# The layer norm's 1/std by three Newton steps on VectorE, in place of Sqrt on ScalarE and a reciprocal

**Chip, cores, metric.** One core of a Trainium2 chip. The metric is the device time of one execution in microseconds (us); the profiles' spans are about 1.8 us shorter.

## The reference, cut to what matters

```python
def _attn_ref(q, k, v, tau):                      # 8 batches, 8 heads, 576 tokens, head size 64
    scores = scale * np.matmul(q, k.transpose(0, 1, 3, 2))
    thresh = np.max(scores, axis=-1, keepdims=True) - tau
    scores = np.where(scores >= thresh, scores, -1000000000.0)
    ... softmax, then attn @ v

def _moe_ref(x, g_ln, w_ch1, w_ch2):              # x: (8, 576, 512), the attention's output
    mu = np.mean(x, axis=-1, keepdims=True)
    var = np.mean((x - mu) ** 2, axis=-1, keepdims=True)
    xn = (x - mu) / np.sqrt(var + 1e-06) * g_ln
    ch = np.maximum(xn @ w_ch1, 0.0) @ w_ch2      # 512 -> 2048 -> 512
    return (x + ch).astype(np.float32)
```

## The kernel before

The work is 72 *slots* of attention (9 for each batch, about 18.5 us each) and 16 *groups* of 288 tokens of the feed-forward part. TensorE runs matmuls of a group between the matmuls of the slots; each slot has four quarters in which such steps are issued. 1/std is a factor of a whole token, so it is applied after the second matmul, and may come late. The tiles that matter: `sc` (scores, PSUM), `em` (attention weights, turned by way of DRAM: `et` to `scr` to `em`), `hidden` (the 2048 features, evicted by ScalarE from one of two PSUM buffers), `rb` (1/std). L numbers in the profiles are lines of the whole kernel.

```python
def exponentials():
    ...
    for h in range(2):
        nc.vector.tensor_reduce(out=neg[:, i], in_=sc[h]..., op=ALU.max, negate=True)        # L372
        nc.gpsimd.tensor_scalar(out=thr[:, i], in0=neg[:, i], ...)
    for i in range(4):
        if i == 2:
            yield es, thr
        nc.scalar.activation(es[:, i], blocks[i], func=AF.Exp, bias=neg[:, i : i + 1])       # L383

def weights(es, thr):
    for i in range(4):
        nc.vector.scalar_tensor_tensor(out=es[:, i], in0=blocks[i], scalar=thr..., in1=es[:, i], ...)  # L389, masking
    nc.vector.reciprocal(den, den)
    for i in range(4):
        nc.gpsimd.tensor_scalar(out=es[:, i], in0=es[:, i], scalar1=den[:, i : i + 1], ...)  # L395, dividing

def ffn_steps(g):
    for d in range(ND):
        ...                                       # four products into p1
        nc.scalar.activation(hidden[:, d], p1, func=AF.Relu)                                 # L587
        yield 2
        ...
        if d == 8:
            var = ps_ff.tile([128, TOK], F32, tag="ff", name="var")
            product(var, lhsT=avg_sb, rhs=sq[:, 0], start=True, stop=True)
            rb = ffn.tile([128, TOK], F32, tag="rb", bufs=2, name="rb")
            nc.scalar.activation(rb, var, func=AF.Sqrt, bias=eps_sb)                         # L598
            aside.append(lambda: nc.vector.reciprocal(rb, rb))                               # L599
            yield 1
    ...

# one slot n, cut to its order
scores(b, s)
rest = exponentials(); es, thr = next(rest)       # maxima and two exponentials
...; second_part(n, 0); next(rest, None)          # quarter 0 of the group's steps, two exponentials
...; run_all(aside); ...; second_part(n, 1)
weights(es, thr)
run_all(aside); ...; second_part(n, 2)
scr = turn_blocks(s, es)                          # L453 and the write to DRAM; fetched in the next slot
...; run_all(aside); ...; second_part(n, 3); tick(4)
run_all(aside)
```

`run_all(aside)` runs what is in the list at that moment; what is appended meanwhile waits for the next call.

Of the kernel before, what the change touches and what calls it, by code (L numbers as in the profile page):

```python
# [10 lines left out]
I32 = mybir.dt.int32  # L11
I64 = mybir.dt.int64
ALU = mybir.AluOpType
AF = mybir.ActivationFunctionType
# [4 lines left out]
def kernel(  # L19
# [31 lines left out]
    nc = tc.nc  # L51
# [29 lines left out]
    eps_sb = consts.tile([128, 1], F32, name="eps_sb")  # L81
# [13 lines left out]
    def product(out, lhsT, rhs, **flags):  # L95


        for h in range(2):
            r = slice(64 * h, 64 * h + 64)
            nc.tensor.matmul(out[r], lhsT=lhsT[:, r], rhs=rhs, **flags)  # L100
# [20 lines left out]
    def load_v(u):  # L121
# [13 lines left out]
        out=tau_sb, in_=bass.AP(tensor=tau.tensor, offset=tau.offset, ap=[[0, 128], [1, 1]])  # L135
    )
    load_qk(0, (nc.sync, nc.scalar))
    for t in q_diag + rests + v_rest:
# [9 lines left out]
        out=scl_sb, in0=tau_sb, scalar1=0.0, scalar2=SCALE, op0=ALU.is_ge, op1=ALU.mult  # L148
    )
    nc.vector.tensor_scalar(  # L150
        out=low_sb, in0=tau_sb, scalar1=0.0, scalar2=BIG, op0=ALU.is_lt, op1=ALU.mult
    )
    nc.vector.scalar_tensor_tensor(
        out=low_sb, in0=tau_sb, scalar=-1.0, in1=low_sb, op0=ALU.mult, op1=ALU.subtract
# [385 lines left out]
    aside, stores = [], []  # L540
# [7 lines left out]
    def add_to_x(g, m, p2, rb):  # L548
        o = ffn.tile([128, TOK], F32, tag="o", bufs=6, name="o")
        nc.vector.tensor_mul(o, p2, rb)  # L550
        nc.gpsimd.tensor_tensor(out=o, in0=o, in1=groups[g][:, m], op=ALU.add)  # L551
        aside.append(lambda: store(g, m, o))
# [6 lines left out]
    def send(g, m, ot):  # L559
        b, t = divmod(g, 2)  # L560
        for i in range(4):
# [5 lines left out]
                in_=ot[32 * i : 32 * i + 32].rearrange("p (n c) -> p n c", c=32),  # L567
            )

    def ffn_steps(g):  # L570



        xc = centred.pop(g)
        rb = None
        for d in range(ND):
            while conversion.ended < 4 * (d // 4 + 1):
                yield 0
            p1 = ps_ff.tile([128, TOK], F32, tag="ff", name="p1")
            for c in range(NK):  # L580
                product(
                    p1, lhsT=w1_sb[c][:, d * 128 : (d + 1) * 128], rhs=xc[:, c],
                    start=(c == 0), stop=(c == NK - 1),
                )
                if c < NK - 1:
# [3 lines that stand above are left out]
            if d == 1:  # L589
                sq = ffn.tile([128, NK, TOK], F32, tag="sq", bufs=1, name="sq")  # L590
                nc.scalar.activation(sq, xc, func=AF.Square)  # L591
                for c in range(1, NK):
                    nc.gpsimd.tensor_tensor(out=sq[:, 0], in0=sq[:, 0], in1=sq[:, c], op=ALU.add)  # L593
            if d == 8:
                var = ps_ff.tile([128, TOK], F32, tag="ff", name="var")
                product(var, lhsT=avg_sb, rhs=sq[:, 0], start=True, stop=True)
                rb = ffn.tile([128, TOK], F32, tag="rb", bufs=2, name="rb")
                nc.scalar.activation(rb, var, func=AF.Sqrt, bias=eps_sb)  # L598
                aside.append(lambda: nc.vector.reciprocal(rb, rb))  # L599
                yield 1  # L600
        for m in range(NK):
            p2 = ps_ff.tile([128, TOK], F32, tag="ff", name="p2")
            for d in range(ND):
                while conversion.ended < conversion.n1 + d + 1:
                    yield 0
                product(
                    p2, lhsT=w2_sb[:, d, m * 128 : (m + 1) * 128], rhs=hidden[:, d],
                    start=(d == 0), stop=(d == ND - 1),
                )
                if d < ND - 1:  # L610
                    yield 2
            aside.append(lambda m=m, p2=p2: add_to_x(g, m, p2, rb))
            yield 2
# [47 lines left out]
    def group_ready(g):  # L661
        at = ready(g) - 1
        for fn in (mean_of, centre):
            at_quarter(*divmod(at, QUARTERS), fn, g)
        at_quarter(*divmod(at + 1, QUARTERS), lambda: queue.append(ffn_steps(g)))
# [108 lines left out]
```

## Time and profile before

| | before |
|---|---|
| median of the first runs | 1529.1 us |
| TensorE busy | 93% of the span |
| VectorE, ScalarE, GpSimd busy | 55%, 29%, 32% |
| table loads on ScalarE | 32 x 1.283 us |
| TensorE waits for ScalarE's evictions into `hidden` | 23.6 us in 21 places |

TensorE sets the time from 190 us on, so what counts of any other engine is how long it makes TensorE wait. The lines for this stand in the prediction.

### The profile page before, as it was taken

What the parts mean: (1) busy time and instruction counts of PE and PEld (TensorE: products, weight loads), DVE (VectorE), ACT (ScalarE), POOL (GpSimd) and SP (SyncE); (2) the same over time, 40 slices, a digit from 0 to 9 for tenths busy, and PEclk for the clock granted to TensorE, in tenths of its full rate; (3) what the DMA queues carried; (4) which work ended last, traced back from release to release, by engine and by line L of the source; (5) the groups of instructions that cost most, each with busy time, mean ns of one, the idle gap of its engine ahead of it and who ended that gap; (6) DMA issues with size and microseconds to landing.
All of it is one profiled execution on the core that took longest, in us unless ns stands there. A gap on an engine that the chain in (4) does not pass through costs nothing.

```text
span 1527.7 us, 28886 instructions
## 1 busy us (share of the span) xinstructions
PE 1416.8 (93%) x11700; PEld 833.7 (55%) x11700; DVE 837.7 (55%) x1380; ACT 442.2 (29%) x797; POOL 487.7 (32%) x737
## 2 busy tenths in 40 slices
PE   3557899999999999999999999999999999999998
PEld 1335455565555555565555655565555655565554
DVE  5877855555654566455664556455654556545210
ACT  3445531323132322314132232313222231313120
POOL 4667443222332323132331323223232323222100
PEclk8777899999999999999999999999999999999999
DMA  9611237455764577555774567645774567545300
GB/s 221 163 39 57 68 82 165 120 136 149 173 164 125 135 171 176 135 137 148 170 169 118 147 154 175 153 125 138 160 169 125 145 152 174 141 125 136 101 9 16
DMA packets 460693, 205.07 MB, mean 134 GB/s; under 512 B 275024, under 2 KB 420176, under 8 KB 460560
## 3 DMA queue, kind: packets, MB, share of 16 engines
q1 hardware_dynamic: 458160, 202.93, 54.4%
q8 instruction: 92, 1.51, 0.4%
q10 hardware_dynamic: 2368, 0.30, 0.2%
q14 instruction: 41, 0.34, 0.1%
q0 software_dynamic: 32, 0.00, 0.0%
HBM read 119.41 MB, written 83.76 MB: 133 GB/s over the span
## 4 chain that ended last, share of the span: by engine, by line
PE 83%; ACT 5%; DVE 5%; POOL 2%; issue 2%; SPq 1%; DMA 1%; POOLq 0%; ACTq 0%; DVEq 0%
PE p L100 62%; PE sc L492 10%; PE sc L359 8%; ACT e L383 4%; DVE neg L372 3%; PE sc L100 2%; POOL e L395 1%; DVE e L389 1%; SPq L112 1%; ACT hidden L587 1%; PE mean L100 1%; ACT L383 0%; DMA v_rest<-in_v_dram 0%; ACT em L423 0%; PE tr L429 0%
## 5 line engine op out<-in xcount | busy, mean ns | idle before, releaser
L100 PE MATMUL p<-xc,w 128*64 128x288 f32 x4096 | 528.5, 414 | 24.9 <-ACT hidden L587 23.6
L100 PE MATMUL p<-hidden,w 128*64 128x288 f32 x4096 | 514.2, 407 | 0.0
L100 PEld LDWEIGHTS p<-xc,w 128*64 128x64 f32 x4096 | 293.5, 139 | 239.5 <-ACT hidden L587 39.0
L100 PEld LDWEIGHTS p<-hidden,w 128*64 128x64 f32 x4096 | 291.2, 137 | 198.4 <-issue 1.4
L372 DVE TENSOR_REDUCE neg<-sc 128x2 f32<-128x1152 f32 x144 | 189.4, 1352 | 339.8 <-PE sc L359 270.0
L395 POOL TENSOR_SCALAR e<-e,den 128x576 f32<-128x576 f32 x288 | 227.3, 806 | 282.9 <-DVE den L393 263.1
L383 ACT ACTIVATE e<-sc,neg 128x576 f32<-128x576 f32 x288 | 192.7, 742 | 289.0 <-DVE neg L372 272.1
L389 DVE SCALAR_TENSOR_TENSOR e<-sc,thr,e 128x576 f32<-128x576 f32 x288 | 219.1, 813 | 26.7 <-ACT e L383 26.2
L453 DVE STREAM_TRANSPOSE et<-e 128x1152 f32<-128x1152 f32 x112 | 153.1, 1372 | 72.5 <-POOL e L395 61.5
L587 ACT ACTIVATE hidden<-p 128x288 f32<-128x288 f32 x256 | 105.1, 415 | 278.2 <-PE p L100 276.1
L359 PE MATMUL sc<-kT,qT 64*128 64x512 f32 (+3 forms) x1024 | 154.3, 439 | 22.7 <-DVE e L389 10.9
L376 POOL TENSOR_SCALAR thr<-neg,low_sb 128x2 f32<-128x2 f32 x144 | 40.3, 280 | 374.2 <-DVE neg L372 374.2
L492 PE MATMUL sc<-em,v_in 128*64 128x256 f32 (+1 forms) x1536 | 149.1, 340 | 4.8 <-DVE e L389 4.4
L359 PEld LDWEIGHTS sc<-kT,qT 64*128 64x128 f32 x1024 | 86.1, 191 | 106.2 <-issue 79.9
L492 PEld LDWEIGHTS sc<-em,v_in 128*64 128x64 f32 x1536 | 97.4, 144 | 49.2 <-DVE e L389 7.1
L509 ACT COPY x<-sc 128x256 f32<-128x256 f32 x64 | 23.9, 373 | 320.5 <-PE sc L492 320.4
L550 DVE TENSOR_TENSOR o<-p,rb 128x288 f32<-128x288 f32 x64 | 28.3, 442 | 123.1 <-PE p L100 123.1
L551 POOL TENSOR_TENSOR o<-o,x 128x288 f32<-128x288 f32 x64 | 51.1, 798 | 131.6 <-DVE o L550 131.3
L518 POOL TENSOR_TENSOR sum<-sum,x 128x256 f32<-128x256 f32 (+1 forms) x64 | 32.2, 502 | 108.2 <-ACT x L509 105.7
L593 POOL TENSOR_TENSOR sq<-sq 128x288 f32<-128x288 f32 x48 | 38.7, 807 | 45.8 <-ACT sq L591 43.3
L492 PE MATMUL sc<-rest,v_rest 128*64 128x256 f32 (+1 forms) x384 | 49.3, 336 | 0.0
L599 DVE RECIPROCAL rb<-rb 128x288 f32<-128x288 f32 x16 | 31.2, 1953 | 30.3 <-ACT rb L598 29.9
(107 smaller groups left out, 656.1 us busy)
## 6 DMA issues: line engine op xcount, KB each, us to landing
scr<-et SPq DMA_DIRECT2D x252, 288.0 KB, 5.1
em<-scr SPq DMA_DIRECT2D x63, 1024.0 KB, 5.9
q_in<-in_q_dram SPq DMA_DIRECT2D x128, 72.0 KB, 3.4
out_dram<-ot SPq DMA_DIRECT2D x256, 36.0 KB, 4.1
k_in<-in_k_dram SPq DMA_DIRECT2D x124, 72.0 KB, 2.7
v_in<-in_v_dram SPq DMA_DIRECT2D x64, 128.0 KB, 4.3
rest<-scr SPq DMA_DIRECT2D x63, 128.0 KB, 5.9
w<-in_moe_w_ch_dram SPq DMA_DIRECT2D x12, 512.0 KB, 4.8
```

The costliest lines, as they stand in the source:

```text
L100: nc.tensor.matmul(out[r], lhsT=lhsT[:, r], rhs=rhs, **flags)
L359: nc.tensor.matmul(sc[h][:, at : at + n], lhsT=qT[r, half, j * 128 : (j + 1) * 128], rhs=kT[r, o : o + n], start=True, stop=True,)
L372: nc.vector.tensor_reduce(out=neg[:, i], in_=sc[h][:, : 2 * S].rearrange("p (j n) -> p j n", j=2), axis=AXL.X, op=ALU.max, negate=True,)
L376: nc.gpsimd.tensor_scalar(out=thr[:, i], in0=neg[:, i], scalar1=-1.0, scalar2=low_sb, op0=ALU.mult, op1=ALU.add,)
L383: nc.scalar.activation(es[:, i], blocks[i], func=AF.Exp, bias=neg[:, i : i + 1])
L389: nc.vector.scalar_tensor_tensor(out=es[:, i], in0=blocks[i], scalar=thr[:, i : i + 1], in1=es[:, i], op0=ALU.is_ge, op1=ALU.mult, accum_o ...
L395: nc.gpsimd.tensor_scalar(out=es[:, i], in0=es[:, i], scalar1=den[:, i : i + 1], scalar2=1.0, op0=ALU.mult, op1=ALU.mult,)
L453: nc.vector.transpose(et[:, :, 64 * h : 64 * h + 64].rearrange("p n (j c) -> p j n c", j=2), es[:, 2 * h : 2 * h + 2].rearrange("p j (n c) ...
L492: nc.tensor.matmul(dst[64 * h : 64 * h + 64], lhsT=vt[:, c, h, :] if c < J else vr[:, h, :], rhs=pick(em[:, c] if c < J else er, hp, h), s ...
L551: nc.gpsimd.tensor_tensor(out=o, in0=o, in1=groups[g][:, m], op=ALU.add)
L587: nc.scalar.activation(hidden[:, d], p1, func=AF.Relu)
L593: nc.gpsimd.tensor_tensor(out=sq[:, 0], in0=sq[:, 0], in1=sq[:, c], op=ALU.add)
```

## The change

In the profile before, each Sqrt has a load of function tables in front of it (16), and so has the exponential that follows (15 times). A load takes 1.283 us. The intent is to do without both: ScalarE only adds the bias (Identity), and VectorE finds 1/sqrt from a guess on the float's bits and three Newton steps. Each step is put into the list of side work by the one before it, so the three parts land in three places.

```diff
+    def root(y, x, t, step=0):
+        if step == 0:
+            nc.vector.tensor_scalar(
+                out=y.bitcast(I32), in0=x.bitcast(I32), scalar1=-0.5, scalar2=float(0x5F3759DF),
+                op0=ALU.mult, op1=ALU.add,
+            )
+        nc.vector.scalar_tensor_tensor(
+            out=t, in0=y, scalar=-0.5, in1=y, op0=ALU.mult, op1=ALU.mult
+        )
+        nc.vector.tensor_mul(t, t, x)
+        nc.vector.scalar_tensor_tensor(out=y, in0=t, scalar=1.5, in1=y, op0=ALU.add, op1=ALU.mult)
+        if step < 2:
+            aside.append(lambda: root(y, x, t, step + 1))
 ...
-                nc.scalar.activation(rb, var, func=AF.Sqrt, bias=eps_sb)
-                aside.append(lambda: nc.vector.reciprocal(rb, rb))
+                nc.scalar.activation(sq[:, 1], var, func=AF.Identity, bias=eps_sb)
+                aside.append(lambda: root(rb, sq[:, 1], sq[:, 2]))
```

## The prediction

> **What bounds the kernel now.** I read the busy shares first, then the slices, the chain of waits, the waits by engine, and last the timeline around the sixteen square roots (one for each group of 288 tokens). The page, in that order:
>
> ```profile
> PE 1416.8 (93%) x11700; PEld 833.7 (55%) x11700; DVE 837.7 (55%) x1380; ACT 442.2 (29%) x797; POOL 487.7 (32%) x737
> ...
> PE   3557899999999999999999999999999999999998
> ...
> PE p L100 62%; PE sc L492 10%; PE sc L359 8%; ACT e L383 4%; DVE neg L372 3%; PE sc L100 2%; POOL e L395 1%; DVE e L389 1%; SPq L112 1%; ACT hidden L587 1%; PE mean L100 1%; ACT L383 0%; DMA v_rest<-in_v_dram 0%; ACT em L423 0%; PE tr L429 0%
> ```
>
> TensorE is at nine tenths from the sixth slice (190 us) to the end; only the start leaves it idle. In the stretch from 230 to 1414 us it is busy for 1160.4 of 1184 us, at a granted clock of 1.00. The chain runs through matmuls for over four fifths. So a change on ScalarE and VectorE is worth only the TensorE idle time it removes or adds. What is touched, from the groups of instructions:
>
> ```profile
> L598 ACT ACT_TABLE_LOAD x16 | 20.5, 1283 | 0.3
> L383 ACT ACT_TABLE_LOAD x15 | 19.2, 1283 | 43.8 <-DVE neg L372 43.8
> ...
> L599 DVE RECIPROCAL rb<-rb 128x288 f32<-128x288 f32 x16 | 31.2, 1953 | 30.3 <-ACT rb L598 29.9
> ...
> L598 ACT ACTIVATE rb<-var,eps_sb 128x288 f32<-128x288 f32 x16 | 8.0, 502 | 0.2
> ```
>
> That is 39.7 us of table loads and 31.2 us of reciprocals, on engines that are 29% and 55% busy. How much of it TensorE feels, the waits say:
>
> ```profile
> PE p L100 <- ACT hidden L587: 23.6, 21, 2.0
> ```
>
> In 21 places the first-layer matmuls wait until ScalarE has evicted an earlier product into `hidden` (two PSUM buffers turn there). In the timeline the 21 places are of three kinds. Seven are like this one, where a table load is part of the delay:
>
> ```profile
> 890.88 2.62 DVE L372 TENSOR_REDUCE neg<-sc 128x2 f32<-128x1152 f32 x2 [4.87 <-PE sc L359]
> ...
> 892.32 1.28 ACT L383 ACT_TABLE_LOAD   x1 [3.27 <-DVE neg L372]
> ...
> 893.61 1.38 ACT L383 ACTIVATE e<-sc,neg 128x576 f32<-128x576 f32 x2
> ...
> 894.88 0.41 ACT L587 ACTIVATE hidden<-p 128x288 f32<-128x288 f32 x1
> ...
> 895.34 6.04 PE L100 MATMUL p<-xc,w 128*64 128x288 f32 x48 [0.53 <-ACT hidden L587]
> ```
>
> The exponential table is fetched back only when the maximum has arrived, then two exponentials, then the eviction; TensorE sits 0.53 us (first number of a row: start, second: length; in brackets the idle time before it). Fourteen are of this kind:
>
> ```profile
> 968.82 2.64 ACT L383 ACTIVATE e<-sc,neg 128x576 f32<-128x576 f32 x4 [3.29 <-DVE neg L372]
> ...
> 971.33 0.43 ACT L587 ACTIVATE hidden<-p 128x288 f32<-128x288 f32 x1
> ...
> 971.77 1.28 ACT L598 ACT_TABLE_LOAD   x1
> 971.81 9.19 PE L100 MATMUL p<-xc,w 128*64 128x288 f32 x60 [1.97 <-ACT hidden L587]
> ```
>
> Here the wait is over four exponentials in front of the eviction; the load for Sqrt comes after it. Every second group has a gap of 1.97 us of this kind and one of 0.51 us some 19 us earlier, with no load near: 7 x 2.48 = 17.4 us, which the change doesn't touch. The rest, 23.6 - 17.4 = 6.2 us, is the seven of the first kind: five of 0.53 us and two of 1.79 us.
>
> [...] the load begins 0.03 us after its predecessor's end. [...] relu and copies follow both loads without one of their own. So Identity in place of Sqrt should leave one load in the program. [...] the trace's 128x288 operations have 442. [...] its two-input operations on 128x512 (L243) took 0.69 us at best and 1.81 at worst.
>
> **The change part by part.** *ScalarE* loses 16 + 15 loads, 39.7 us, and keeps 16 evictions of 0.50 us [...]. Expected: 442.2 - 39.7 = 402.5 us busy. On TensorE this is worth:
> - five gaps of 0.53 us: the eviction comes 1.28 us earlier, more than the gap: 5 x 0.53 = 2.7 us;
> - two gaps of 1.79 us (ending at 373.5 and 1243.9 us), where four exponentials stand before the eviction: only the 1.28 of the load goes, 2 x 1.28 = 2.6 us;
> - one load at 181.0 us in the start, ahead of the copies that a transpose waits 2.44 us for: 1.3 us;
> - a wait of 0.09 us beside the Sqrt load in every second group: 8 x 0.09 = 0.7 us.
>
> Together at most 7.2 us, 0.47% of 1529.2.
>
> *VectorE* loses the reciprocal, 1.95 us, and gets ten instructions per group: one tensor-scalar on the bits, and three times three with two tensors. The latter are 0.44 to 0.46 us each. The first has one source in SBUF; the like of it in the conversion (L239) took 0.42 us for 512 elements at best, so for 288 some 0.3 us. Sum 9 x 0.45 + 0.3 = 4.4 us in place of 1.95: 16 x 2.4 = 39 us more, 837.7 to about 877 us, 57% of the span, without contention. It still isn't the bound. What counts is where the three parts fall. They enter the queue of side work one after another, so each lands at another point of the slots (a slot is one block of attention, about 18.5 us):
> - Groups like the one at 971.8: the first part follows the attention weights, the second the block transposes, the third ends the slot. The transposes end perhaps 1.3 us later. The weights that are fetched from that slot were issued at 986.13 with a median landing of 5.9 us, and used at 1000.45: 8 us to spare. Nothing lost.
> - Groups like the one at 882.2 (Sqrt late in its slot): the first part is at the slot's end, where VectorE then idles 4.87 us: free. The second, 3 x 0.45 = 1.35 us, falls into the next slot just ahead of the masking of the weights (L389), which there starts as soon as VectorE is free (895.81): 1.35 us later. The third comes after the masking, beside GpSimd's four divisions by the sum (L395, 0.73 us each), before the transposes. VectorE waits there 1.6 us for GpSimd anyway, so without contention the third part is hidden; [...]
>
> So in every second group the turned weights reach the next slot 1.35 to 2.65 us later. They go out to DRAM and come back, and the fetch usually waits for the write:
>
> ```profile
> SPq L468 <- DMA scr<-et: 145.0, 69, 4.7
> ```
>
> In the slot after 903.5 the fetch was issued at 911.85, lands near 917.8, and TensorE uses it at 920.33: 2.5 us to spare. Over the seven such slots after the start I find from issue, landing and first use 3.6, 2.0, 2.5, 2.4, 1.2, 3.9 and 1.4 us to spare. In some the fetch itself waits a little behind other loads, and takes up 0.4 to 1.6 us of the delay. A delay of 1.35 us overruns only the last, by about 0.6 us (with TensorE 0.5 us earlier, [...]); one of 2.65 us overruns five, by 1.05, 0.2, 0.3, 0.5 and 1.9: 4 us.
>
> [...] *Buffers:* the bias sum and scratch go into slices of `sq` that are dead by then; the next group writes `sq` only some 60 us later. The first product that needs `rb` is ready some 20 us after the root begins, three parts or not (last group: 1478.4 against 1498.24).
>
> Sum: -7.2 + 0.6 to 4, that is 3.2 to 6.6 us gained. I take 4.7 us: 1524.5 us.
>
> **The rivals.** (1) *Nothing gained*: the second and third parts of the root, lengthened by GpSimd, make TensorE wait for the fetched weights as long as it no longer waits for ScalarE; or they delay the conversion in the first 230 us, where TensorE is busy 66.75 of 75 us in the stretch from 155 on. For it: spare times of 1.2 to 2 us. Against: half the groups have 8 us to spare. 1527 to 1531 us. (2) *The whole 40 us of loads come back*, as if ScalarE were on the path: about 1490 us. Against it: the waits of TensorE on ScalarE are 23.6 us in all, and 17.4 of them have no load in front. (3) *VectorE becomes the bound*, 39 us more work: 1560 us. Against: it idles 4 to 8 us in front of nearly every maximum. (4) *The full 7 us*: contention is small and every spare time suffices: 1522 us.
>
> **Range and chances.** Between (4) and (1): 1521.5 to 1529.5. Faster by 2% would need 30 us where TensorE's waits on the touched parts are 7; slower by 2% would need nearly 2 us lost in each group: 0.005 and 0.01.
>
> **What would show it.** One table load; ScalarE near 402 us busy. The gaps of 0.53 us gone, those of 1.79 down to about 0.5, so TensorE's waits on `hidden` near 18.4 us; the fourteen others unchanged. Root operations of 0.45 us at their shortest, longer where GpSimd is at work; VectorE at 877 to 900 us. New, short waits of TensorE in front of the weighted values (L492), in the slots after every second group. Wrong would be the account if these waits are absent and the time still doesn't fall, if the gaps of 0.53 us stay, or if Identity brings loads of its own.

## The result, and the profile after

The first four runs took 1523.75, 1524.8, 1526.81 and 1528.45 us: median 1525.8 against 1529.1. The ratio was 0.998, 95% interval 0.9962 to 0.9997. (A ratio is the mean time of one kernel's fast runs over that of the other's of the same rounds, so it isn't quite the ratio of the medians.) Six more runs later gave a median of 1527.89, from 1523.45 to 1530.1, ratio 0.9993 (0.998 to 1.0007). So the change gains 1 to 3 us of 1529, about 0.1 to 0.2%, and the second batch alone cannot tell it from nothing.

The busy line of the page after:

```profile
PE 1413.7 (93%) x11700; PEld 834.5 (55%) x11700; DVE 892.2 (59%) x1524; ACT 401.6 (26%) x766; POOL 491.1 (32%) x737
```

ScalarE lost 40.6 us and 31 instructions (the loads; one is left, at L247), VectorE gained 54.5 us. The waits of TensorE, longest first (total in us, times, longest one):

```profile
PE p L100 <- ACT hidden L603: 18.2, 16, 2.0
...
PE sc L492 <- DVE et L453: 1.4, 1, 1.4
```

The first is the wait for evictions, 23.6 us before: five gaps of 0.53 us are gone, and the two of 1.79 us are 0.45. The second is new, in front of the weighted values. VectorE's `et` is named there, but that transpose only ended at the same moment and is not what this matmul reads. The matmul reads `em`, fetched from DRAM, and in the trace the fetch landed 0.14 us before it, 7.8 us after its issue (the median is 5.9). In another profile of the same kernel the same wait is named by its transfer:

```profile
PE sc L492 <- DMA em<-scr: 0.5, 1, 0.5
```

Now the second group of a batch at the place that the prediction shows of before (timeline: start, length, engine, line, what, in brackets the idle time before it):

```profile
880.97 0.31 DVE L574 TENSOR_SCALAR rb<-sq 128x288 int32<-128x288 int32 x1 [0.19 <-ACT sq L614]
881.32 0.46 DVE L578 SCALAR_TENSOR_TENSOR sq<-rb 128x288 f32<-128x288 f32 x1
...
883.29 0.46 DVE L581 TENSOR_TENSOR sq<-sq 128x288 f32<-128x288 f32 x1
...
890.36 1.37 ACT L383 ACTIVATE e<-sc,neg 128x576 f32<-128x576 f32 x2 [3.29 <-DVE neg L372]
...
891.62 0.41 ACT L603 ACTIVATE hidden<-p 128x288 f32<-128x288 f32 x1
...
893.89 0.46 DVE L578 SCALAR_TENSOR_TENSOR sq<-rb 128x288 f32<-128x288 f32 x1
...
895.25 0.81 DVE L389 SCALAR_TENSOR_TENSOR e<-sc,thr,e 128x576 f32<-128x576 f32 x1
```

The exponential follows its maximum at once. Of the root, two parts lie at the end of the slot (from 880.97), where VectorE is free, and the third (from 893.89) directly in front of the masking, which it puts off by 1.36 us.

To see where time comes and goes I compared, slot by slot, when the first maximum of the slot starts in the two traces. From 250 us on the profiled run after gains 0.75 us in each of five second groups and 1.34 in two, 6.4 us together, and 0.06 us beside each former Sqrt load. It loses 1.62 us in one slot (the wait of 1.4), and 0.5 us in all in three others. The larger steps that are left, two of about +1.69 us and one of -1.70, come from something else: the granted clock. The trace shows intervals of 3.413 us at half clock, each costing 1.7 us of matmuls. Between 250 and 1500 us there are three of them before (at 624, 798 and 972 us) and four after. In the second profile of the changed kernel there are seven. Four intervals more are 6.8 us, over twice what the change gains. Before 250 us the profiled run gains 2.3 us, the second profile of the same kernel 0.7.

### The profile page after: what moved, and what is told of

It is laid out like the page before. It is cut to its first block, busy times and chain, and to the rows that moved or that the text cites. A ratio compares the mean times of both kernels' runs of the same rounds, so it can differ in the third digit from the quotient of the medians.

```text
span 1522.0 us, 28782 instructions
## 1 busy us (share of the span) xinstructions
PE 1413.7 (93%) x11700; PEld 834.5 (55%) x11700; DVE 892.2 (59%) x1524; ACT 401.6 (26%) x766; POOL 491.1 (32%) x737
## 4 chain that ended last, share of the span: by engine, by line
PE 82%; DVE 6%; ACT 4%; POOL 3%; issue 2%; DMA 2%; SPq 1%; POOLq 0%; ACTq 0%; DVEq 0%
PE p L100 61%; PE sc L492 10%; PE sc L359 8%; ACT e L383 3%; DVE neg L372 2%; POOL e L395 2%; PE sc L100 2%; DVE e L389 1%; SPq L112 1%; DMA v_rest<-in_v_dram 1%; PE mean L100 1%; DVE w L266 0%; DVE w L239 0%; DMA scr<-et 0%; ACT hidden L603 0%
## 5 line engine op out<-in xcount | busy, mean ns | idle before, releaser
L100 PE MATMUL p<-xc,w 128*64 128x288 f32 x4096 | 525.3, 413 | 19.0 <-ACT hidden L603 18.2
L395 POOL TENSOR_SCALAR e<-e,den 128x576 f32<-128x576 f32 x288 | 230.6, 817 | 287.1 <-DVE den L393 271.2
L383 ACT ACTIVATE e<-sc,neg 128x576 f32<-128x576 f32 x288 | 192.7, 741 | 337.0 <-DVE neg L372 337.0
L518 POOL TENSOR_TENSOR sum<-sum,x 128x256 f32<-128x256 f32 (+1 forms) x64 | 32.5, 508 | 92.8 <-ACT x L509 90.3
L429 PE MATMUL tr<-ident,e 128*64 128x128 f32 x36 | 9.1, 405 | 41.8 <-ACT em L423 34.1
```

What stands on the lines that cost most here:

```text
L100: nc.tensor.matmul(out[r], lhsT=lhsT[:, r], rhs=rhs, **flags)
```

## The experiments

Twelve runs (eleven new kernels and the changed one again), all with five rounds, four to six executions each. The four batches of experiments ran on different chips. Runs in one batch share the runs of before: 1529.26 us in the first batch, 1528.13 in the second, 1528.35 in the third, 1528.92 in the fourth (medians; the single runs lie between 1526.16 and 1531.11).

| run | median us | ratio, 95% interval | correct |
|---|---|---|---|
| ScalarE's half alone | 1522.3 | 0.996 (0.9948 to 0.9972) | no |
| VectorE's half alone | 1526.88 | 0.9995 (0.9982 to 1.0008) | no |
| root in one piece | 1525.94 | 0.9984 (0.9972 to 0.9997) | yes |
| changed kernel again | 1527.89 | 0.9993 (0.998 to 1.0007) | yes |
| root ahead of the masking | 1554.54 | 1.0178 (1.0155 to 1.0201) | yes |
| root behind the masking | 1553.41 | 1.0164 (1.015 to 1.0178) | yes |
| load moved, nothing else | 1522.38 | 0.9963 (0.9949 to 0.9976) | yes |
| before, whole quarters | 1519.0 | 0.9945 (0.9933 to 0.9958) | yes |
| one piece, whole quarters | 1507.83 | 0.9869 (0.9855 to 0.9882) | yes |
| load moved, whole quarters | 1510.86 | 0.9882 (0.9869 to 0.9896) | yes |
| changed kernel, whole quarters | 1510.3 | 0.9876 (0.986 to 0.9892) | yes |
| one piece, first group later | 1522.82 | 0.9957 (0.9944 to 0.9971) | yes |

The theory: the two table loads cost TensorE some 7 us, and the root gives a part back by waits for fetched weights. The rivals: it is the amount of VectorE's work and not its place that costs, or the loads need not go for the gain.

### 1. The halves

ScalarE's half alone:

```diff
-                nc.scalar.activation(rb, var, func=AF.Sqrt, bias=eps_sb)
+                nc.scalar.activation(rb, var, func=AF.Identity, bias=eps_sb)
```

> The ScalarE half of the change alone: Identity in place of Sqrt, so no table is swapped, and the one reciprocal stays on VectorE (the result is wrong on purpose: 1/var instead of 1/std). If all of the gain is in the table loads and VectorE's extra work only takes some of it back: one table load, no wait of TensorE in front of the weighted values in the steady part, each second group about 0.75 us (five times) or 1.34 us (twice) earlier than before, in all 7 to 8 us: 1521 to 1522 us. If the gain came from the root instead: near 1529.

Measured 1522.3 us (1521.51 to 1523.34), as expected; one load; no wait for fetched weights. The slots show the five steps of 0.75 us and the two of 1.28. So taking the loads away is worth 7 us, and the changed kernel gets less than half of it.

These 7 us are not simply the gaps, though. Of the 7.5 us between the two profiled spans, 4.6 are gained before 250 us. There the load at 181 us (in the prediction's sum at 1.3 us) is gone, and so are 1.41 us of TensorE's wait behind it, and an interval of half clock from 183.5 to 190.4 us, which made the matmuls after the wait slower. Before, then with ScalarE's half alone:

```profile
184.17 1.06 PE L429 MATMUL tr<-ident,e 128*64 128x128 f32 x4 [2.44 <-ACT em L423]
185.16 12.48 PE L100 MATMUL p<-xc,w 128*64 128x288 f32 x80
```

```profile
182.38 0.63 PE L429 MATMUL tr<-ident,e 128*64 128x128 f32 x4 [1.03 <-ACT em L423]
182.94 9.92 PE L100 MATMUL p<-xc,w 128*64 128x288 f32 x80
```

From 250 us on the gaps give 6.3 us, and five intervals of half clock in place of three take 3.4 of it back. The clock's gain at the start and its loss later nearly cancel in these two profiles. Both are in part chance (part 5 tells why): in the changed kernel a wait of 2.84 us at the same place brings no interval.

VectorE's half alone is the changed kernel with one word put back:

```diff
-                nc.scalar.activation(sq[:, 1], var, func=AF.Identity, bias=eps_sb)
+                nc.scalar.activation(sq[:, 1], var, func=AF.Sqrt, bias=eps_sb)
```

> The VectorE half alone: Sqrt and its tables stay on ScalarE, and the ten instructions run on its output in place of the reciprocal (the result is wrong on purpose). If the extra work on VectorE costs TensorE waits for the fetched weights in one or two slots: 0.5 to 3 us slower than before, 1529.5 to 1532 us. If VectorE's work is free: 1529. If the root gained anything by itself: below 1528.

Measured 1526.88 us (1525.57 to 1531.95). This was the surprise: no loss. Its profile has the waits for fetched weights (2.5 us in two places), and all 31 loads are back. Yet the gaps that I had laid at the loads' door did not come back:

```profile
PE p L100 <- ACT hidden L603: 18.2, 16, 2.0
...
PE sc L492 <- DMA em<-scr: 2.5, 2, 1.9
```

ScalarE's timeline in this run tells why:

```profile
887.66 0.41 ACT L603 ACTIVATE hidden<-p 128x288 f32<-128x288 f32 x1 [1.53 <-PE p L100]
888.09 1.28 ACT L383 ACT_TABLE_LOAD   x1
891.36 1.37 ACT L383 ACTIVATE e<-sc,neg 128x576 f32<-128x576 f32 x2 [1.99 <-DVE neg L372]
```

The load for Exp starts 0.02 us after the eviction and is done 1.99 us before the exponential has its maximum. In the kernel before, the load itself sat idle for the maximum (3.27 us, in the prediction's lines). The totals show the same: before, the 15 loads at L383 wait 43.8 us for maxima, here 21.4, and L383 has 61 semaphore instructions of its own before and 54 here. Why the wait moved from the load to the exponential no run isolates. What follows for the theory doesn't depend on it: with all 31 loads back, TensorE waits 18.2 us for evictions as in the changed kernel, against 23.6 before, so these loads cost it time by where they stand.

### 2. Only the load's place

```diff
                 nc.scalar.activation(rb, var, func=AF.Sqrt, bias=eps_sb)
+                nc.scalar.activation(dummy, eps_sb, func=AF.Exp)       # a 128x1 tile
```

> The kernel before with one exponential of a 128x1 tile right behind each Sqrt, so that the exponential's table is fetched back there, in ScalarE's idle time, and not behind the wait for the next maximum. All 31 table loads, Sqrt and the reciprocal stay (the result is right). The run with VectorE's half alone kept every load, and still each second group came 0.75 or 1.34 us earlier, since there the second load ran before the maximum's wait. If the gain is only that one load's place: the seven gaps of 0.53 and 1.79 us close, 6 to 6.5 us less in the steady part, 1521.5 to 1523.5 us. If the loads themselves must go for it: 1529.

Measured 1522.38 us (1521.06 to 1523.76): the same as with no loads at all (1522.3), with 33 loads in the program and ScalarE busier than before (445.2 us against 442.2):

```profile
L599 ACT ACT_TABLE_LOAD x16 | 20.5, 1283 | 0.3
L600 ACT ACT_TABLE_LOAD x16 | 20.5, 1283 | 0.3
```

The slots show -0.75 and -1.28 us at the very places of the run without loads, the same 4.6 us before 250 us and the same five intervals of half clock. So what the change gains on ScalarE is not the 40 us of loads but the place of seven of them in the steady part and one at the start, and one line on ScalarE gains it without the root.

### 3. Where the root stands

In one piece:

```diff
         if step < 2:
-            aside.append(lambda: root(y, x, t, step + 1))
+            root(y, x, t, step + 1)
```

> The changed kernel with the ten instructions of the root in one piece instead of three. In every second group all of it then lies at the slot's end, where VectorE idles 4 us, and nothing comes in front of the masking of the weights in the next slot. If the loss is that third part in front of the masking: as fast as the ScalarE half alone within 1 us, 1521 to 1522, with no wait of TensorE for the fetched weights and a smaller spread from run to run than the changed kernel. If it is the amount of VectorE work and not its place: as the changed kernel, about 1525.5.

Measured 1525.94 us (1525.85 to 1526.49). Half of the expectation held: no wait for fetched weights anywhere, the full steps of -0.75 and -1.34 us in each second group, and a spread of 0.6 us in place of 4.7. But the time missed by 3.6 us. The slot comparison puts the loss before 210 us, in the first group, whose root falls into the conversion of the weights. There GpSimd works almost without pause (168.58 to 175.59 us in the changed kernel), and the first part of the first root looks like this:

```profile
170.69 1.37 DVE L574 TENSOR_SCALAR rb<-sq 128x288 int32<-128x288 int32 x1 [0.67 <-ACT sq L614]
...
172.10 1.43 DVE L578 SCALAR_TENSOR_TENSOR sq<-rb 128x288 f32<-128x288 f32 x1
...
173.57 0.87 DVE L581 TENSOR_TENSOR sq<-sq 128x288 f32<-128x288 f32 x1
...
174.47 1.44 DVE L582 SCALAR_TENSOR_TENSOR rb<-sq,rb 128x288 f32<-128x288 f32 x1
...
180.42 2.62 DVE L372 TENSOR_REDUCE neg<-sc 128x2 f32<-128x1152 f32 x2
```

Four operations that take 1.7 us elsewhere take 5.1 here. In GpSimd's pause from 175.59 to 177.81 us one of the second part (at 177.49) takes 0.45; the next, at 177.98, beside GpSimd's L257, takes 1.43. And the maximum starts at 180.42 although its scores are ready 2 us earlier. Maximum, exponentials, copies of the weights by ScalarE and TensorE's transposes follow one on another there, so the delay reaches TensorE: it waits 2.84 us near 184 us after, 3.49 in one piece, and 1.03 with ScalarE's half alone. In one piece:

```profile
183.92 0.72 PE L429 MATMUL tr<-ident,e 128*64 128x128 f32 x4 [3.49 <-ACT em L423]
```

The run that tests this moves that one root:

```diff
+                if g == 0:
+                    at_quarter(SLOTS - 1, 2, root, rb, sq[:, 1], sq[:, 2])
+                else:
                     aside.append(lambda: root(rb, sq[:, 1], sq[:, 2]))
```

> The root in one piece (1525.9 us), but the first group's root one slot later, behind the masking at about 190 us, away from the weight conversion. In the run in one piece TensorE waits 3.49 us near 184 us for ScalarE's copies, against 1.03 in the run with ScalarE's half alone, and an interval of half clock follows. If that is the whole rest of its 3.6 us over the half alone: that wait near 1 us, no interval of half clock there, 1521.5 to 1523 us. If the root costs TensorE elsewhere: 1525 to 1526.

Measured 1522.82 us (1519.26 to 1523.72). The wait near 184 us is 1.03 us again:

```profile
181.97 0.63 PE L429 MATMUL tr<-ident,e 128*64 128x128 f32 x4 [1.03 <-ACT em L423]
```

The interval of half clock at 184.3 us, which the version in one piece has behind this wait, is gone too. Of the 2.2 us between the two profiled spans (1524.1 and 1521.9), 2.1 are gained before 250 us. So both losses of the root are named: the first group among the conversions, and its third part in front of the masking. With both avoided the root is within 0.5 us of the half without it (1522.82 and 1522.3, of different batches), and its work on VectorE is as good as free.

### 4. More of the suspected cost

All three parts go into a list of their own, which is emptied directly ahead of the masking, or directly behind it:

```diff
+        run_all(roots)          # one kernel: here
         weights(es, thr)
+        run_all(roots)          # the other: here instead
         run_all(aside)
```

> A larger dose of the suspected cost: all ten instructions of the root in one piece directly in front of the masking of the weights. In every second group they delay the masking, and so the write and the fetch of the turned weights, by about 4.4 us instead of 1.4. From the spare times before (3.6, 2.0, 2.5, 2.4, 1.2, 3.9 and 1.4 us) and what the fetch absorbs, TensorE should wait 1 to 4 us in each of seven slots, some 15 us: 1532 to 1540 us. If VectorE's place in the slot doesn't matter: as the changed kernel, about 1525.5.

> The same ten instructions directly behind the masking, where GpSimd divides by the sums (four operations of 0.73 us) and the block transposes follow. Without contention the root of 4.4 us runs beside GpSimd and the transposes end some 2.8 us later: waits of TensorE of about 5 us in all, 1525 to 1528 us, root operations of 0.46 us. [...] root operations of up to 1.2 us or divisions of over 0.8 us, the transposes 4 to 5.5 us later: 1532 to 1545 us.

Measured 1554.54 us (1550.93 to 1562.11) and 1553.41 us (1551.4 to 1554.1): the direction was right, the sizes too small. Ahead of the masking, TensorE's waits for the fetch are close to the 15 us expected; behind it they are more:

```profile
PE sc L492 <- DMA em<-scr: 14.4, 7, 2.9
```

```profile
PE sc L492 <- DMA em<-scr: 22.7, 7, 4.4
```

What I had left out are the intervals of half clock, of which there are eight in the second of these profiles (six in the first) in place of three: 5 x 1.7 = 8.5 us. With the 7 us of the loads off, 22.7 + 8.5 - 7 = 24.2 us; the span is 24.1 us longer than before (1551.8 against 1527.7). So close a fit is partly luck: the start alone differs by 1.6 us between the two profiles of the changed kernel. In the first of the two other waits come in as well, 9.0 us in place of 4.4 for the masking itself among them; I did not split that one to the end.

The second run also shows contention by itself, as the root stands beside GpSimd's divisions:

```profile
553.38 3.49 POOL L395 TENSOR_SCALAR e<-e,den 128x576 f32<-128x576 f32 x4 [4.57 <-DVE den L393]
553.50 0.92 DVE L578 SCALAR_TENSOR_TENSOR sq<-rb 128x288 f32<-128x288 f32 x1
...
554.45 0.88 DVE L581 TENSOR_TENSOR sq<-sq 128x288 f32<-128x288 f32 x1
...
555.37 0.88 DVE L582 SCALAR_TENSOR_TENSOR rb<-sq,rb 128x288 f32<-128x288 f32 x1
556.29 0.88 DVE L578 SCALAR_TENSOR_TENSOR sq<-rb 128x288 f32<-128x288 f32 x1
...
557.20 0.46 DVE L581 TENSOR_TENSOR sq<-sq 128x288 f32<-128x288 f32 x1
```

While GpSimd divides, VectorE's operations of two tensors (L578 to L582) take 0.88 to 0.92 us in place of 0.46, and the four divisions 3.49 us in place of 2.9; when it is done (556.9), they are 0.46 again, but for one at 558.19 beside GpSimd's L518 (0.93). So both are slower beside each other. But by their durations they did not go strictly in turn: four divisions and four such operations would take 4 x (0.73 + 0.46) = 4.8 us that way, and here they took 3.8 (553.38 to 557.17). In the run ahead of the masking all of them took 0.46 us.

### 5. The spread, and the intervals of half clock

The changed kernel unaltered:

> The changed kernel once more, for a second profile and its spread. If the spread (1523.75 to 1528.45) is fetches that come just in time or just too late: 1524 to 1528 again, and the second profile shows the wait for the fetched weights in another number of slots (0 to 4) than the first one's one. If it is the granted clock: the runs' times follow the listed clock, about 1.7 us for each interval of 3.4 us at half clock in the steady part.

Measured 1523.45 to 1530.1 us. Its profile has a shorter wait for the fetch (0.5 us by name) and seven intervals of half clock in the steady part, against four in the first profile. The clock in the run list is only a mean over the span with the start in it, and does not order the runs by time (1528.49 us at 0.968, 1526.02 at 0.966). The intervals themselves are seen in the profiled runs alone, so the spread is put down to them by two profiles, not by all ten executions.

Where do they come from? Before, the three in the steady part follow TensorE's gaps of 1.97 us in the first group of a batch; so do the others in all profiles, apart from those that follow the longer waits of part 4. The clock of before around the gap that ends at 971.81 us (columns: stretch, its length, busy time of the engines, granted clock, DMA share, GB/s):

```profile
967.00:971.80 4.80, 2.84 (x26) 1.42 (x22) 4.13 (x7) 2.97 (x6) 0.54 (x2) 1.00 0.54 138
971.80:976.00 4.20, 4.19 (x22) 2.22 (x24) 4.11 (x9) 1.99 (x3) 2.35 (x4) 0.59 0.52 195
```

After the gap the clock is 0.59 over 4.2 us: one interval at a half.

The traces also show why one gap is followed by an interval and another isn't. In each trace all intervals start whole multiples of 3.413 us after one another, so they mark a grid of windows of that length. I took TensorE's idle time in every such window from 250 to 1500 us, in all fourteen traces. The 54 intervals there each follow a window with at least 1.96 us idle. Of the other 5088 windows only one has that much; the next has 1.94. So in these traces a gap of 1.97 us brought an interval where it lay whole in one window. In the kernel before, those that end at 622.81, 797.31 and 971.81 us do; the other four are cut by a border into about 1.75 and 0.2 us, and bring none, nor do the two gaps of 1.79 us. How many intervals these executions got thus depended on where their windows happened to lie.

To test the gaps themselves I removed them. A gap comes about because quarter 0 ends in the middle of a product, so that the product's eviction is queued behind all four exponentials:

```diff
-        while queue and (owed >= 0.5 or got == 1 and i == QUARTERS - 1):
+        while queue and (owed >= 0.5 or got == 1 and i in (0, QUARTERS - 1)):
```

> The kernel before, with the first quarter of each slot also made to finish the product it has begun, so that its eviction stands between the second and third exponential and not behind the fourth. For the theory that the intervals of half clock in the steady part start at TensorE's idle time of 1.97 us in every second group: those seven gaps close (14 us), and with them the 3 to 7 intervals, 1.7 us each: 1505 to 1515 us, at most one interval of half clock after 230 us. If the intervals come by themselves: 1512 to 1517, with 3 to 7 intervals left. If the forced end breaks the balance of the slots: over 1529.

Measured 1519.0 us (1518.58 to 1521.17). The gaps are 0.7 us, and no interval of half clock is left between 250 and 1500 us. So the intervals belong to the gaps. The time is above the expected band, as the gaps were not closed whole and a new wait opened where Sqrt's load stands between two evictions:

```profile
PE p L100 <- ACT hidden L587: 12.1, 21, 0.7
...
PE p L100 <- ACT rb L598: 6.4, 7, 0.9
```

Now the load in front of Sqrt, which was hidden in the kernel before, is on TensorE's path. That is where the change should come into its own:

> The root in one piece and the first quarter made whole: should beat both kernels if both gains add: 6 to 7 us below the kernel before with whole quarters, 1498 to 1508 us.

> The two steps without the root: Sqrt and all loads stay, the exponential's table comes back right behind Sqrt, and the first quarter is made whole. In the kernel before with whole quarters TensorE waits seven times 0.9 us for Sqrt's output (6.4 us), since its own load stands in front of it. If loads matter only where they stand: the seven gaps of the exponential's load close, those 6.4 us stay: about 1513 us. If it equals the root's version with whole quarters: 1508.

> The changed kernel as it is (root in three parts) with whole quarters. If the third part in front of the masking still makes TensorE wait for fetched weights now that TensorE is faster: some waits for the fetch, 1 to 4 us and half-clock intervals over the version with the root in one piece: 1509 to 1514 us. If the parts don't matter: 1508.

Measured 1507.83 us (root in one piece), 1510.86 (load moved) and 1510.3 (the change as it is, 1508.82 to 1513.31), each with whole quarters and none with an interval of half clock in the steady part. In the one with the load moved the wait for Sqrt stays at 6.4 us in seven places, in the two with the root it is gone; the change as it is waits 4.3 us in four places for fetched weights, in one piece 0.5 us in one. On this schedule the change is worth 8.7 us (1519.0 to 1510.3, of two batches) and in one piece 11.2, more than the 6 to 7 expected, against 1 to 3 us and 3.3 on the schedule before. Two things make it worth more here: the wait for Sqrt (6.4 us), which this schedule brought up and the root takes away, and the intervals of half clock, of which the changed kernel had one to four more in its profiles (1.7 to 6.8 us) and now has none. How they share the difference was not split. The version in one piece with whole quarters is the best one measured, correct, 1.3% below the kernel before.

The version with the load moved came out faster than the 1513 expected, and close to the root's, because of the start: its slot near 250 us begins at 245.6 us, against 251.4 in one piece with whole quarters, where TensorE still waits 3.12 us near 185 us for the first group's root (1.03 with the load moved). After that slot the root in one piece gains 7.3 us more. Whole quarters together with the later first root was not run.

## Why the prediction was right, and where it was off

The forecast of 1524.5 us, range 1521.5 to 1529.5, holds the median of the result, 1525.8, and that of the second batch, 1527.89. Two of the second batch's six runs lie above the range. The mechanism was right in the main: a few waits of TensorE behind table loads go, and some for fetched weights come. That the number came so close is partly luck, as the sum left out the root's cost at the start and the half-clock intervals.

- **Bound and ceiling: right, the ceiling with luck.** TensorE's wait for evictions was forecast at 18.4 us and is 18.2; the gain that the loads can give at 7.2 us at most, and ScalarE's half alone gives 7.0 (1529.26 - 1522.3). But its start gave 4.6 us in the profile, where the sum had 1.3 for the load there, and two more intervals of half clock took 3.4 away. The rivals of 40 us gained or lost fell with the first profile.
- **ScalarE and VectorE busy: right.** 402.5 forecast, 401.6 measured; 877 to 900 forecast, 892.2 measured. The 16 evictions take the 0.50 us forecast: 0.501 with Identity, 0.502 with Sqrt (medians).
- **Five gaps of 0.53 us: too small.** Each second group comes 0.75 us earlier; where the 0.22 us beyond the gap come from was not shown. The two with 1.28 gain 1.34. These terms were 5.3 us of the sum; 6.4 are measured.
- **Cause of these gaps: only half right.** I read that the loads had to go. The run with one small exponential has every load and the same gain. The prediction's own lines showed it: the load had 3.27 us of idle time *in front of it*, waiting for the maximum.
- **The parts' places: off by one.** The prediction had the first part at the slot's end, the second ahead of the masking, the third beside GpSimd. The variance is ready one call of the side work earlier, so two parts lie at the slot's end and the third ahead of the masking. The delay is 1.36 us, the lower of the two cases, without the contention. The upper case, 2.65 us, was the author's estimate: 1.3 us more if GpSimd's four divisions and VectorE's three operations went strictly in turn, which no trace shows (part 4: 3.8 us, where strict turns would take 4.8). Its cost was said to be 0.6 us at the least, of which 0.45 follow from the 1.35, the 0.5 and the 1.4 us, and the rest was the author's estimate; 2.1 us are measured in four slots of the first profile, 1.5 in four of the second (the slots' steps once more). The spare times were shorter than I read them: TensorE comes 0.75 us earlier, not 0.5, and one fetch took 7.8 us where I reckoned with the median of 5.9. That one made the long wait, in a slot for which the prediction found over 2 us to spare and forecast none. In the last slot, the one that it named, TensorE did not wait: 0.73 us were left.
- **The root at the start: left out of the sum.** It was named as part of the first rival, but given no time, though the conversion's own operations (L243) took 0.69 to 1.81 us before. In the first group contention makes four operations 3.4 us longer and TensorE waits 1.8 us more (2.84 against 1.03). The run that moves that root settles it: 1525.94 to 1522.82.
- **Noise: not foreseen.** Intervals of half clock, 1.7 us each, vary in number: three before, four and seven in the two profiles of the changed kernel. The forecast's range was worked out from waits alone.

What stays open: what sets where the windows of 3.413 us lie in an execution, the one window of 1.96 us that no interval followed, and why the wait for the maximum moved from the load to the exponential in part 1.

## What to carry to other kernels

Ask of a table load not how long it takes but what stands in front of and behind it: where it waits with its activation for an input, a small activation of the same function in idle time moves it out of the way (here 1528.35 to 1522.38 us). Work that is put on an idle engine was free here only where nothing that TensorE reads soon stood behind it in that engine's queue (the root in one piece, with the first one moved: 1522.82 us; ahead of the masking: 1554.54); read the queue at each place where it lands, the start included. Before judging a change of a few tenths of a per cent, remove the larger gaps of TensorE first: here they brought half-clock intervals (1.7 us each, three to seven between 250 and 1500 us in the profiles of the two kernels, none with whole quarters) that blurred the result. They also hid a wait: without them Sqrt's load stood in TensorE's way (6.4 us in seven places), and the same change was worth about 9 us in place of 1 to 3.
